# Fixed issue order on every engine, staged loads and software-pipelined slots in a fused linear-attention and gMLP block

## The chip, the cores and the metric

The kernel runs on one core of one Trainium2 chip. The metric is the device time of one execution in microseconds (us); lower is better. A *profile* is one execution with the hardware profiler on. Its *span* runs from the first to the last instruction. Executions come in two states: some are a few per cent longer than the fastest of the same kernel, whatever the kernel; those over 1.5% longer are called slow.

In the lines of the profile PE is TensorE (matmuls) and PEld its weight loads, DVE is VectorE, ACT ScalarE, POOL GpSimd and SP SyncE. A `q` after an engine's name, as in ACTq or SPq, marks an instruction that issues work from its queue, here DMA transfers. `out<-in` names the tiles, and L566 is line 566 of that run's kernel. A *bank* is a piece of PSUM, the memory that matmuls write; an *eviction* copies a result out of it. *Clock* is the granted TensorE clock as a share of full speed.

## The reference, cut to what matters

Sequence 2048, model width 448, 16 heads of 28, hidden width 896 for each half of the gMLP, all bf16.

```python
mod = (silu(c) @ w_mod)            # six vectors of 448: sa, ca, ga, sb, cb, gb
h = layernorm(x) * (1 + ca) + sa
q, k, v = split(h @ wqkv)
phi = lambda t: concat(softmax(t @ w_phi), softmax(-(t @ w_phi)))      # per head
kv, z = phi(k).T @ v, phi(k).sum(0)
x = x + ga * ((phi(q) @ kv / (phi(q) @ z + 1e-6)) @ wo)
h = layernorm(x) * (1 + cb) + sb
z1, z2 = split(gelu(h @ w_in)); z2 = layernorm(z2)
g = w_sp @ z2 + b_sp                # a 2048 x 2048 product over the sequence
x = x + gb * ((z1 * g) @ w_out)
```

## The kernel before

The sequence is cut into 16 tiles of 128 rows, and the program has four stages. The **start** loads the weights, computes silu(c) and the modulation vectors, and folds w_phi and (1 + ca) into the K weights; for this it lays w_phi out as a block-diagonal matrix, BD. The **K stage** computes k, v and the sum over phi(k) for each tile, and the q features in between. The **middle** goes through slots: `num` (attention numerator), `wo` (output projection, second norm), `z2` and `z1`. The **gate stage** multiplies by w_sp and w_out. Norms go as follows: VectorE computes mean and variance, GpSimd raises the variance to the power -1/2 (`rstd`), VectorE computes `nmr` = -mean * rstd, GpSimd applies both, and a DMA transpose makes the result a matmul operand (hT for the first norm, h2T for the second).

A scheduler orders the instructions of each engine; the program text gives only the dependences and a priority. The parts that matter, with cuts marked `# ...`:

```python
# head of the program: every load, from two queues
nc.scalar.dma_start(out=wm1[:], in_=wmod_v[:, :, 0:960])
nc.sync.dma_start(out=x_sb[:, 0:4, :], in_=xv[:, 0:4, :])
# ... Wv on SP; wk_raw and four blocks of BD on ScalarE
for st in range(1, NST):
    nc.sync.dma_start(out=x_sb[:, st * 4:(st + 1) * 4, :], in_=xv[:, st * 4:(st + 1) * 4, :])
load_rows(nc.scalar, wq_raw[:], A_wqkv[:, 0:D])
# ... wmg, wo_s, wm2 on ScalarE
load_rows(nc.scalar, win_s[:], B_w_in)
# ... wmg, wout_s on ScalarE
nc.scalar.dma_start(out=bsp[:], in_=B_b_sp.partition_broadcast(P))
# ...
nc.scalar.activation(out=e[:], in_=cT[:], func=ACT.Exp, scale=-1.0)      # the start of silu(c)

# PSUM: six single banks and one pair
def bank(name):  return psp.tile([P, 512], F32, name=name, tag="B", bufs=6)
def bank2(name): return psp.tile([P, 2, 512], F32, name=name, tag="A", bufs=1)

# middle
for j in range(NT + 7):
    if j < NT: num(j)
    # ... z1 of the tiles that are ready
    if 0 <= j - 2 < NT: wo(j - 2)          # ends with the second norm and its h2T transpose
    if 0 <= j - 4 < NT: z2(j - 4)          # two single banks, two gelus
    if 0 <= j - 5 < NT: z2norm(j - 5)
    if j >= NT:
        for n in ((j - NT) * 2, (j - NT) * 2 + 1):
            if n < 8: load_wsp(2 + n // 4, n % 4)    # w_sp pieces, transposed on the SP queue
```

Of the kernel before, what the change touches and what calls it, by code (L numbers as in the profile page):

```python
# [15 lines left out]
P = 128  # L16
D = 448
# [457 lines left out]
KD = [P, P, P, D - 3 * P]  # L475
HP = 4
# [4 lines left out]
def fast_path(tc, A_x, A_wqkv, A_w_phi, A_wo, B_w_in, B_w_sp, B_b_sp, B_w_out, c, w_mod, out, flag):  # L481


    nc = tc.nc
# [5 lines left out]
    wspA = tc.alloc_tile_pool(name="f_wspA", bufs=1)  # L490
# [3 lines left out]
    def bank(name):  # L494
        return psp.tile([P, 512], F32, name=name, tag="B", bufs=6)

    def bank_bf(name):
        return psp.tile([P, 1024], BF, name=name, tag="B", bufs=6)

    def bank2(name):  # L500
        return psp.tile([P, 2, 512], F32, name=name, tag="A", bufs=1)

    ident = persist.tile([P, P], BF, name="f_ident")
    make_identity(nc, ident[:])
# [8 lines left out]
    sbcol = persist.tile([P, KC], BF, name="f_sbcol")  # L513
    cb1 = persist.tile([P, KC], F32, name="f_cb1")
    xpad = [persist.tile([P, 512], BF, name=f"f_xpad{r}") for r in range(6)]
    opad = [persist.tile([P, 512], BF, name=f"f_opad{r}") for r in range(3)]
# [7 lines left out]
    wq_raw = aph.tile([P, KC, D], BF, name="f_wq_raw")  # L524
    BD = aph.tile([CB, 4, CB], BF, name="f_BD")
# [5 lines left out]
    vring = [aph.tile([P, H, DH + 1], BF, name=f"f_vaug{r}") for r in range(3)]  # L531

    sm = tc.alloc_tile_pool(name="f_sm", bufs=3)


    c_row = aph.tile([1, D], BF, name="f_c_row")
    nc.sync.dma_start(out=c_row[:], in_=c)
    xv = A_x[0].rearrange("(n p) d -> p n d", p=P)
    wmod_v = w_mod.rearrange("(k p) n -> p k n", p=DC)
    nc.scalar.dma_start(out=wm1[:], in_=wmod_v[:, :, 0:960])  # L540
    nc.sync.dma_start(out=x_sb[:, 0:4, :], in_=xv[:, 0:4, :])
# [4 lines left out]

    load_rows(nc.sync, Wv[:], A_wqkv[:, 2 * D:3 * D])
    nc.vector.memset(BD[:], 0.0)
    load_rows(nc.scalar, wk_raw[:], A_wqkv[:, D:2 * D])
    phiv = A_w_phi.rearrange("(g l) d f -> l d g f", l=4)  # L550
    with nc.allow_non_contiguous_dma(reason="small w_phi blocks"):
        for hl in range(4):
            nc.scalar.dma_start(out=BD[hl * DH:(hl + 1) * DH, :, hl * DH:(hl + 1) * DH], in_=phiv[hl])
    for st in range(1, NST):
        nc.sync.dma_start(out=x_sb[:, st * 4:(st + 1) * 4, :], in_=xv[:, st * 4:(st + 1) * 4, :])
    load_rows(nc.scalar, wq_raw[:], A_wqkv[:, 0:D])
    nc.scalar.dma_start(out=wmg[:, :, 0:D], in_=wmod_v[:, :, 2 * D:3 * D])
    load_rows(nc.scalar, wo_s[:], A_wo)
    nc.scalar.dma_start(out=wm2[:], in_=wmod_v[:, :, 3 * D:3 * D + 960])
    load_rows(nc.scalar, win_s[:], B_w_in)  # L560
    nc.scalar.dma_start(out=wmg[:, :, D:2 * D], in_=wmod_v[:, :, 5 * D:6 * D])
    nc.scalar.dma_start(out=wout_s[:], in_=B_w_out.rearrange("(k p) n -> p k n", p=P))
    nc.scalar.dma_start(out=bsp[:], in_=B_b_sp.partition_broadcast(P))


    nc.gpsimd.memset(mhalf[:], -0.5)  # L566
    for r in range(6):
        nc.gpsimd.memset(xpad[r][:, D:512], 0.0)
        nc.gpsimd.memset(xpad[r][:, D:D + 1], 1.0)
    for r in range(3):  # L570
        nc.gpsimd.memset(opad[r][:, D:512], 0.0)
        nc.gpsimd.memset(pring[r][:, 2 * D:2 * D + 16], 0.0)
        nc.gpsimd.memset(vring[r][:, :, DH:DH + 1], 1.0)
    nc.gpsimd.memset(Wq[:, :, D:D + 16], 0.0)
    sapad = aph.tile([P, KC, 65], BF, name="f_sapad")
    sbpad = persist.tile([P, KC, 65], BF, name="f_sbpad")
    nc.gpsimd.memset(sapad[:], 0.0)
    nc.gpsimd.memset(sbpad[:], 0.0)
    ones = aph.tile([P, 1], BF, name="f_ones")
    nc.gpsimd.memset(ones[:], 1.0)  # L580
    with nc.allow_low_precision("a 0/1 mask is exact in bf16"):
        nc.vector.tensor_reduce(out=mask[:], in_=ident[:].rearrange("p (k h) -> p h k", h=HP), axis=AX.X, op=ALU.add)
    for s in range(2):
        nc.vector.tensor_copy(out=KVbd[:, s, :, :, 29], in_=mask[:].unsqueeze(1).to_broadcast([P, 4, HP]))


    ct_ps = bank_bf("ct_ps")
    for kk in range(KC):
        nc.tensor.transpose(ct_ps[0:DC, 2 * kk:2 * kk + 1], c_row[0:1, kk * DC:(kk + 1) * DC], ident[0:1, 0:1])
    ctv = ct_ps[0:DC, 0:8].rearrange("p (k t) -> p k t", t=2)[:, :, 0]  # L590
    cT = aph.tile([DC, KC], F32, name="f_cT")
    nc.vector.tensor_copy(out=cT[:], in_=ctv)
    e = aph.tile([DC, KC], F32, name="f_e")
# [3 lines left out]
    scol = aph.tile([DC, KC], BF, name="f_scol")  # L597
    nc.vector.tensor_tensor(out=scol[:], in0=e[:], in1=cT[:], op=ALU.mult)  # L598

    def colform(wm, pad, one_plus, tagn):  # L600
        cf = bank("cf" + tagn)
        for j in range(8):
            jv, m = divmod(j, 4)
            for kk in range(KC):
                nc.tensor.matmul(cf[:, j:j + 1], lhsT=wm[:, kk, jv * D + m * P:jv * D + m * P + P],  # L605
                                 rhs=scol[:, kk:kk + 1], start=(kk == 0), stop=(kk == KC - 1))
        nc.vector.tensor_copy(out=pad[:, :, 64], in_=cf[:, 0:4])
        nc.vector.tensor_scalar(out=one_plus[:], in0=cf[:, 4:8], scalar1=1.0, scalar2=None, op0=ALU.add)
        nc.vector.memset(one_plus[64:65, 3:4], 1.0)

    ca1 = aph.tile([P, KC], F32, name="f_ca1")

    def fold_T(wraw, wT):
        for g in range(4):
            tps = bank_bf("tps")
            for m in range(KC):
                nc.tensor.transpose(tps[0:CB, m * P:m * P + KD[m]], wraw[0:KD[m], m, g * CB:(g + 1) * CB],
                                    ident[0:KD[m], 0:KD[m]])
            if g % 2 == 0:
                nc.vector.tensor_copy(out=wT[:, g, 0:D], in_=tps[0:CB, 0:D])  # L620
            else:
                nc.scalar.copy(out=wT[:, g, 0:D], in_=tps[0:CB, 0:D])

    def fold_W(wraw, wT, W):
# [5 lines left out]
        nc.vector.tensor_copy(out=wT[:, :, D], in_=sa_ps[0:CB, 0:4])  # L630
        for m in range(KC):
            M = P if m < 3 else 65
            pf = bank("pf")
            for g in range(4):
                nc.tensor.matmul(pf[0:M, g * CB:(g + 1) * CB], lhsT=wT[:, g, m * P:m * P + M], rhs=BD[:, g, :],
                                 start=True, stop=True)
            dst = W[0:M, m, 0:D].rearrange("p (g f h) -> p g h f", g=4, h=HP)
            srcv = pf[0:M, 0:D].rearrange("p (g h f) -> p g h f", g=4, h=HP)
            if m % 2 == 0:
                nc.scalar.activation(out=dst, in_=srcv, func=ACT.Copy, scale=ca1[0:M, m:m + 1])  # L640
            else:
                nc.vector.tensor_scalar(out=dst, in0=srcv, scalar1=ca1[0:M, m:m + 1], scalar2=None, op0=ALU.mult)

# [7 lines left out]

    xr = [0]

    def ln_tail(mv, n, src, idx, tagp, dst):

        rstd = sm.tile([P, 4], F32, tag=tagp + "rs")
        nc.gpsimd.tensor_scalar(out=rstd[:, 0:n], in0=mv[:, 0:n, 1], scalar1=LN_EPS, scalar2=None, op0=ALU.add)
        nc.gpsimd.tensor_tensor(out=rstd[:, 0:n], in0=rstd[:, 0:n], in1=mhalf[:, 0:n], op=ALU.pow)
        nmr = sm.tile([P, 4], F32, tag=tagp + "nm")
        nc.vector.scalar_tensor_tensor(out=nmr[:, 0:n], in0=mv[:, 0:n, 0], scalar=-1.0, in1=rstd[:, 0:n], op0=ALU.mult, op1=ALU.mult)  # L660
        for t in range(n):
            xp = xpad[xr[0] % 6]
            xr[0] += 1
            nc.gpsimd.tensor_scalar(out=xp[:, 0:D], in0=src(t), scalar1=rstd[:, t:t + 1], scalar2=nmr[:, t:t + 1],  # L664
                                    op0=ALU.mult, op1=ALU.add)
            nc.sync.dma_start_transpose(out=dst(t), in_=xp[:])  # L666

    def ln1(st):
        mv = sm.tile([P, 4, nc.vector.BN_AGGR_DIM], F32, tag="l1mv")
        for t in range(4):  # L670
            stats = sm.tile([P, nc.vector.BN_STATS_DIM], F32, tag="l1st")
            nc.vector.bn_stats(out=stats[:], in_=x_sb[:, st * 4 + t, :])
            nc.vector.bn_aggr(out=mv[:, t, :], in_=stats[:])
        ln_tail(mv, 4, lambda t: x_sb[:, st * 4 + t, :], None, "l1",
                lambda t: hT[:, :, (st * 4 + t) * P:(st * 4 + t + 1) * P])

    ln1(0)
    colform(wm1, sapad, ca1, "a")
    wT = aph.tile([CB, 4, D + 1], BF, name="f_wTk")
    fold_T(wk_raw, wT)  # L680
    bv = bias_row(sapad, Wv, 0, D)
    for kk in range(KC):
# [3 lines left out]
    fold_W(wk_raw, wT, Wk)  # L686
# [3 lines left out]
    kvacc = bank2("kvacc")  # L690

    def kv_proj(i):
        k_ps = bank("k_ps")
        v_ps = bank("v_ps")
        for kc in range(KC):
            K = P if kc < 3 else 65
            nc.tensor.matmul(k_ps[:, 0:D], lhsT=hT[0:K, kc, i * P:(i + 1) * P], rhs=Wk[0:K, kc, :], start=(kc == 0), stop=(kc == KC - 1))  # L697
        for kc in range(KC):
            K = P if kc < 3 else 65
# [312 lines left out]
```

## Time and profile before

| | before |
|---|---|
| timed runs, median (range) | 363.83 us (363.71 to 364.49) |
| profiled run | 372.96 us, span 371.1, state slow |
| first K matmul | 66.4 us |
| K stage, to the first `num` matmul | 66.4 us |
| middle, to the first w_sp matmul | 113.1 us |
| gate stage | 125.2 us |

The first K matmul is the first matmul of the first K tile: its k in the kernel before, its v in the changed one. The prediction below shows the strip of busy tenths, ScalarE's start and the table of stretches. One more view was used to check the stages, the list of what PE waited for: the waiting operation and its line, the releaser, then the total in us, the number of waits and the longest.

```profile
PE cfa L605 <- DVE f_scol L598: 54.2, 1, 54.2
PE num L829 <- DVE t L843: 10.6, 8, 3.5
PE x_ps L856 <- DMA oT<-f_opad: 7.6, 4, 3.1
PE z_ps L877 <- DMA h2T<-f_xpad: 4.3, 2, 2.9
```

The first line is the start: one wait of 54.2 us for silu(c). The second is the middle, where `num` has a single pair of banks and waits for VectorE to empty it.

### The profile page before, as it was taken

The numbers are of one execution on the slowest core, as the hardware profiler recorded it, in microseconds if no ns is written. First come the engines' busy times: TensorE is split into PE (matmuls) and PEld (weight loads), VectorE is DVE, ScalarE is ACT, GpSimd is POOL, SyncE is SP. The second block draws the span as 40 slices with busy tenths as digits, with TensorE's granted clock in tenths as the row PEclk, the third lists the DMA queues.
The fourth block names the chain that finished last, engine by engine and source line by source line (L and its number), as shares of the span: only waits on it lengthen the run. The fifth ranks groups of instructions, "written<-read, shape, count | busy, mean of one in ns | idle before, by whom it ended". The sixth has DMA issues, their size and how long they took to land. (4 is left out here: it accounts for less than half of the span.)

```text
span 371.1 us, 4240 instructions
## 1 busy us (share of the span) xinstructions
PE 275.0 (74%) x1506; PEld 134.6 (36%) x1528; DVE 174.0 (47%) x384; ACT 98.6 (27%) x206; POOL 100.3 (27%) x176
## 2 busy tenths in 40 slices
PE   0000008999969946897879795799999999999992
PEld 0000006665425522333334341244444444444440
DVE  1720003696726745667777764233443334444422
ACT  0000012677718751534445462240000000000000
POOL 2552400345940014754655554000000000000000
PEclk9999999999969996889999997799999999999997
DMA  8999899800000002412222279700000000000001
GB/s 229 269 208 208 166 218 238 108 2 1 2 0 0 2 0 42 73 34 53 42 44 56 42 154 208 165 5 0 0 2 25 25 2 25 25 2 12 27 12 56
DMA packets 69656, 25.81 MB, mean 70 GB/s; under 512 B 60473, under 2 KB 69050, under 8 KB 69626
## 3 DMA queue, kind: packets, MB, share of 16 engines
q1 hardware_dynamic: 64290, 18.76, 25.4%
q10 hardware_dynamic: 5336, 6.69, 8.2%
q8 instruction: 14, 0.23, 0.3%
q14 instruction: 16, 0.13, 0.1%
HBM read 8.92 MB, written 1.84 MB: 29 GB/s over the span
## 5 line engine op out<-in xcount | busy, mean ns | idle before, releaser
L932 PE MATMUL g_ps<-f_wsp,f_z2n 128*128 128x512 bf16 x437 | 98.2, 379 | 0.6
L932 PEld LDWEIGHTS <-f_z2n 128*128 128x128 bf16 x448 | 43.9, 98 | 52.2
L934 DVE TENSOR_TENSOR gb<-g_ps,f_bsp 128x512 f32<-128x512 f32 x28 | 19.4, 692 | 68.6 <-PE g_ps L932 68.6
L605 PE MATMUL cfa<-f_scol,f_wm 112*128 112x1 bf16 x32 | 1.0, 165 | 54.2 <-DVE f_scol L598 54.2
L877 PE MATMUL z_ps<-f_win,h2T 128*128 128x448 bf16 (+1 forms) x128 | 31.3, 391 | 4.3 <-DMA h2T<-f_xpad 4.3
L845 POOL TENSOR_TENSOR f_opad<-t 128x448 bf16<-128x448 bf16 x16 | 16.5, 1033 | 53.6 <-issue 30.4
L898 PE MATMUL z_ps<-h2T,f_win 128*128 128x512 bf16 (+1 forms) x106 | 27.9, 397 | 3.1 <-DMA h2T<-f_xpad 2.6
L664 POOL TENSOR_SCALAR f_xpad<-f_x,rstd,nmr 128x448 bf16<-128x448 bf16 x32 | 22.9, 721 | 21.8 <-DMA f_hT<-f_xpad 13.2
L856 PE MATMUL x_ps<-f_wo,oT 128*128 128x448 bf16 x64 | 18.9, 391 | 7.6 <-DMA oT<-f_opad 7.6
L880 DVE BATCH_NORM_STATS2 stats<-z2g 128x6 f32<-128x448 bf16 x32 | 19.4, 611 | 9.6 <-ACT z2g L879 9.6
L939 PE MATMUL o_ps<-f_wout,f_z1T 128*128 128x448 bf16 x112 | 23.3, 352 | 0.0
L707 DVE TENSOR_REDUCE sums<-f_E 128x32 f32<-128x896 bf16 x16 | 17.3, 1084 | 11.8 <-ACT f_E L703 11.6
L605 PEld LDWEIGHTS <-f_wm 112*128 112x128 bf16 x64 | 2.0, 100 | 54.4 <-issue 50.1
L879 ACT ACTIVATE z2g<-z_ps 128x448 bf16<-128x448 f32 x32 | 17.4, 544 | 14.6 <-PE z_ps L877 14.6
L899 ACT ACTIVATE f_z1T<-z_ps 128x512 bf16<-128x512 f32 x28 | 16.7, 597 | 14.5 <-PE z_ps L898 14.5
L935 DVE TENSOR_TENSOR f_z1T<-gb,f_z1T 128x512 bf16<-128x512 f32 x28 | 19.4, 692 | 1.7 <-DVE gb L934 0.5
L877 PEld LDWEIGHTS <-h2T 128*128 128x128 bf16 (+1 forms) x128 | 13.3, 107 | 17.8 <-DMA h2T<-f_xpad 5.4
L829 PE MATMUL num<-f_KVbd,f_Eq 112*128 112x120 bf16 x128 | 10.5, 232 | 12.3 <-DVE t L843 10.6
L843 DVE TENSOR_TENSOR t<-num,w 128x896 bf16<-128x896 f32 x16 | 17.4, 1087 | 0.4
L697 PE MATMUL k_ps<-f_Wk,f_hT 128*128 128x448 bf16 x64 | 16.6, 380 | 0.2 <-ACT f_Wk L640 0.2
L729 PE MATMUL q_ps<-f_hT,f_Wq 128*128 128x512 bf16 (+1 forms) x59 | 16.6, 396 | 0.3
L898 PEld LDWEIGHTS <-f_win 128*128 128x128 bf16 x112 | 10.9, 100 | 15.3 <-DMA h2T<-f_xpad 3.4
(111 smaller groups left out, 351.3 us busy)
## 6 DMA issues: line engine op xcount, KB each, us to landing
f_x<-in_A_x_dram SPq DMA_DIRECT2D x4, 448.0 KB, 7.0
out_dram<-ot SPq DMA_DIRECT2D x16, 112.0 KB, 1.7
f_wm<-in_w_mod_dram ACTq DMA_DIRECT2D x2, 840.0 KB
f_win<-in_B_w_in_dram ACTq DMA_DIRECT2D x1, 1344.0 KB, 13.3
f_wmg<-in_w_mod_dram ACTq DMA_DIRECT2D x2, 392.0 KB
f_wout<-in_B_w_out_dram ACTq DMA_DIRECT2D x1, 784.0 KB
f_bsp<-in_B_b_sp_dram ACTq DMA_DIRECT2D x1, 512.0 KB, 4.7
f_wk_raw<-in_A_wqkv_dram ACTq DMA_DIRECT2D x1, 336.0 KB, 7.9
```

The source lines that it names most:

```text
L664: nc.gpsimd.tensor_scalar(out=xp[:, 0:D], in0=src(t), scalar1=rstd[:, t:t + 1], scalar2=nmr[:, t:t + 1], op0=ALU.mult, op1=ALU.add)
L707: nc.vector.tensor_reduce(out=sums[:], in_=E[:].rearrange("p s (c f h) -> p (s c) h f", c=4, h=HP), axis=AX.X, op=ALU.add)
L843: nc.vector.tensor_tensor(out=t[:], in0=nv[:, :, :, 0:DH], in1=w[:].unsqueeze(3).to_broadcast([P, 2, H, DH]), op=ALU.mult)
L856: nc.tensor.matmul(x1[:, 0:D], lhsT=oT[0:KD[cc], cc, :], rhs=wo_s[0:KD[cc], cc, :], start=(cc == 0), stop=False)
L877: nc.tensor.matmul(z_ps[:, 0:D], lhsT=h2[0:K, kc, il * P:(il + 1) * P], rhs=win_s[0:K, kc, FH + hf * D:FH + (hf + 1) * D], start=(kc == 0) ...
L879: nc.scalar.activation(out=z2g[:, hf, :], in_=z_ps[:, 0:D], func=ACT.Gelu_apprx_tanh)
L880: nc.vector.bn_stats(out=stats[:, hf, :], in_=z2g[:, hf, :])
L898: nc.tensor.matmul(z_ps[:], lhsT=win_s[0:K, kc, fc * P:(fc + 1) * P], rhs=h2[0:K, kc, :], start=(kc == 0), stop=(kc == KC - 1))
L932: nc.tensor.matmul(g[:], lhsT=z2n[:, s_, fc * P:(fc + 1) * P], rhs=wsp_tiles[tcn][:, s_, :], start=(s_ == 0), stop=(s_ == NT - 1))
L934: nc.vector.tensor_tensor(out=gb[:], in0=g[:], in1=bsp[:, tsl], op=ALU.add)
L935: nc.vector.tensor_tensor(out=z1T[:, fc, tsl], in0=gb[:], in1=z1T[:, fc, tsl], op=ALU.mult)
L939: nc.tensor.matmul(o_ps[:, 0:D], lhsT=z1T[:, fc, t * P:(t + 1) * P], rhs=wout_s[:, fc, :], start=(fc == 0), stop=(fc == FC - 1))
```

## The change

The intent is to take the order out of the scheduler's hands: every engine gets its instructions in the order of the text, so that loads stand where they are needed, and each slot does work whose inputs were made a slot earlier. The diff, cut to its core:

```diff
+    with tc.manual_schedule():                      # around everything below
-    bank: bufs=6      bank2: bufs=1
+    bank: bufs=4      bank2: bufs=2
 # start: only what is needed first; table load ahead of the exponential
-    for st in range(1, NST):
-        nc.sync.dma_start(out=x_sb[:, st * 4:(st + 1) * 4, :], ...)
-    load_rows(nc.scalar, wq_raw[:], A_wqkv[:, 0:D])
-    ...                                             # wmg, wo_s, wm2, win_s, wmg, wout_s, bsp on ScalarE
+    nc.sync.dma_start(out=cT[:], in_=c.rearrange("o (k p) -> p (o k)", p=DC))    # c as columns
+    nc.scalar.activation(out=warm[:], in_=warm[:], func=ACT.Exp)
+    nc.vector.tensor_tensor(out=BD[:]..., in0=phi[:]..., in1=bmask[:]..., op=ALU.mult)   # BD by a mask
 # K stage
+    def loads(i):                                   # on SP, one or two per slot
+        if i == -1: x tiles 4-7, wq_raw
+        elif i == 0: x tiles 8-11, wmg ...
+        ...                                         # to i == 7: bsp
+    for i in range(NT):
+        q_exp of an earlier pair; k_mm(i)
+        l1_stats(i + 4); l1_rstd; l1_apply(i + 3, nc.gpsimd)
+        loads(i); k_norm(i); kv_acc(i - 2); late(i)
+        if i in QS: q_mm(QS[i])                     # two q chunks into a pair of banks
+        if 10 <= i < 14: load_wsp(0, i - 10)
 # middle
-    num(j); z1; wo(j - 2); z2(j - 4); z2norm(j - 5)
+    for j in range(NT + 8):
+        l2_apply(j - 4); num_fin(j - 1); z2_norm(j - 7); wo_mm(j - 3)
+        z2_stats(j - 6); z2_rstd(j - 6); l2_stats(j - 3); z2_mm(j - 5)
+        z1 units; num_mm(j)                         # z2_mm: two halves, a pair of banks, one gelu
+    for tcn in range(1, 4):                         # w_sp after the last h2T
+        for q in range(4): load_wsp(tcn, q)
```

Smaller parts: the folded weights are kept in an order that lets their evictions be contiguous, the second norm's statistics are read from PSUM instead of from the copy, and the scaling of wo and w_in moves from GpSimd to VectorE.

## The prediction

> **What bounds the kernel now.** I read the profile in this order: the forty-slice strip of busy tenths, the ScalarE timeline of the first 58 us, the table of stretches cut where the program changes stage, then the chain that ended last and VectorE's timeline inside one stage.
>
> The strip shows PE idle for the first six slices (9.3 us each) while the DMA engines are 80 to 90% busy, and again thinner in the middle:
>
> ```profile
> PE   0000008999969946897879795799999999999992
> DMA  8999899800000002412222279700000000000001
> ```
>
> The ScalarE timeline says why PE starts so late. All of ScalarE's loads stand ahead of its first computation, exp(-c), and everything PE needs (the modulation columns, then the folded K weights) hangs on that exponential:
>
> ```profile
> 24.80 0.39 ACTq L544 DMA_DIRECT2D f_win<-in_B_w_in_dram  x1
> 40.49 0.47 ACTq L545 DMA_DIRECT2D f_win<-in_B_w_in_dram  x1
> 54.25 0.36 ACTq L563 DMA_DIRECT2D f_bsp<-in_B_b_sp_dram  x1
> 54.64 1.28 ACT L594 ACT_TABLE_LOAD   x1 [54.64 <-DMA f_hT<-f_xpad]
> 55.93 0.21 ACT L594 ACTIVATE f_e<-f_cT 112x4 f32<-112x4 f32 x1
> ```
>
> The reader is to see the gap from 24.80 to 40.49 between two issues: the built program makes a load wait for the transfer eight issues earlier, so the queue advances only as data lands. c itself was in the chip at 2.0 us and the first modulation weight at 6.6 us.
>
> The stretches (fold, K stage, attention/MLP stage, its drain, spatial gate) give each engine's busy time:
>
> ```profile
> 56.50:66.40 9.90, 9.37 (x84) 7.05 (x84) 3.74 (x13) 2.90 (x5) 0.61 (x1) 1.00 1.09 212
> 66.40:132.80 66.40, 61.85 (x428) 33.73 (x433) 42.61 (x66) 44.90 (x88) 27.37 (x23) 0.95 0.10 13
> 132.80:211.50 78.70, 58.50 (x335) 27.41 (x339) 53.62 (x153) 33.83 (x86) 41.57 (x71) 0.91 0.23 44
> 211.50:245.90 34.40, 27.30 (x108) 11.13 (x109) 15.12 (x40) 14.88 (x28) 11.84 (x26) 0.85 0.70 146
> 245.90:371.10 125.20, 117.48 (x550) 54.74 (x559) 47.48 (x72) 0.60 (x1) 0.00 (x0) 0.98 0.05 16
> ```
>
> First figure after the bounds is the length, then PE, PEld, DVE, ACT, POOL busy, the granted clock, DMA share, GB/s. The K stage is PE's (93%). The gate stage is PE's too and nothing in it can be hidden better. The middle is nobody's: PE 74%, VectorE 68%. In it a slot repeats every 5.66 us; VectorE works about 4.35 of that and waits twice for GpSimd's power:
>
> ```profile
> 201.19 0.16 DVE L660 SCALAR_TENSOR_TENSOR nmr<-mv,rstd 128x1 f32<-128x1 f32 x1 [0.73 <-POOL rstd L658]
> 203.12 0.51 DVE L890 TENSOR_SCALAR f_z2n<-z2g,mv,rstd 128x896 bf16<-128x896 bf16 x1 [0.58 <-POOL rstd L885]
> 206.85 0.16 DVE L660 SCALAR_TENSOR_TENSOR nmr<-mv,rstd 128x1 f32<-128x1 f32 x1 [0.73 <-POOL rstd L658]
> ```
>
> The drain is stalled by the queue: small h2T transposes stand on SP behind the big f_wsp ones, and the chain that ended last runs through them:
>
> ```profile
> 229.41 0.04 issue
> 229.45 2.04 SPq L738
> 231.49 0.04 issue
> 231.53 2.13 SPq L738
> ...
> 233.76 2.83 DMA h2T<-f_xpad
> ```
>
> **What the Trainium skill says.** "TensorE: Matmul & The Clock Gate", § Architectural detail, says ScalarE and VectorE are strict first-in first-out. The trace agrees: the table load starts at 54.64, straight after the last issue (54.25 + 0.36). The same page, § What's actually happening, gives PE half rate until about 3.4 us of sustained work and again after an idle window. The trace agrees: in the first K tile 448-column matmuls start 0.37 us apart (66.73 to 67.10), in a steady one 0.19, and the granted clock is 0.50 in 140 to 145 us, after an idle gap. "DMA: Bandwidth & Descriptors", § Issuing engines are not separate DMA queues, says loads started by different engines share the same 16 DMA engines. So moving loads from ScalarE to SP buys no bandwidth (218 GB/s over the first 56 us); it can only free ScalarE and change the order.
>
> **The change part by part**, in the profiled run's time, by stage.
>
> 1. *Start.* ScalarE keeps four issues of its present kind for wm1 and wk_raw, and its table load is moved ahead. c comes as columns, so four transposes go. Before K tile 0 only about 2.1 MB must land; at 218 GB/s that is about 10 us, and wk_raw, early in it, about 8 us (in the profile it took 7.9 us behind a load of twice the size). From there the fold costs what it costs now, 9.9 us: about 18 us for the first K matmul instead of 66.4. **Gain 48 us.**
>
> 2. *K stage.* PE's work is the same: 16 tiles of k, v (8 x 0.19 = 1.5 us) and accumulation (0.42), 64 q matmuls (14 us), folds, gates, bias rows and norms: about 57 us at full clock. The 4.0 us for which PE now waits around 101 to 107 us for the squares on GpSimd go, and q exponentials are paired. Against that, VectorE carries per slot statistics 0.75, sum 1.1, reciprocal 0.35, product 0.8: 3.0 us, plus about 7 us of scaling moved from GpSimd. Banks fall from six single ones to four and evictions wait in VectorE's order, so in slots 1 to 3, with the fold of q, K tile i+1 waits for tile i's exponentials (1.3), normalisation (2.3) and eviction: about 5 us each. The loads for this stage, 6.7 MB and 1.2 MB of transposes, need 36 us at 218 GB/s, and slots 0 to 12 last about 45: close, not binding. Working: slots 0 to 3 20 us, 4 to 11 8 x 3.2 + 2, 12 to 15 13.5, the tail with the last norms and q 7: **68 us, against 66.4: loss 2 us.** It ends near 86.
>
> 3. *Middle.* Two pair banks instead of one let num run ahead. But the order is fixed, and VectorE's last item in a slot (second-norm statistics) releases GpSimd's add and power (0.22 + 0.57 + hand-overs, about 1.05 us), which releases VectorE's first item in the next. VectorE's own starts-to-starts in the slot add to 4.5 us. Slot: 4.5 + 1.05 = **5.55 us, against 5.66**. Fill until slot 7 goes at that pace: num, VectorE chain 2, add 1.05, transpose 2.5 and so on, 23 us. Then 9 slots of 5.55 = 50; slots 16 to 19 without num 5.5 + 3.6 + 3.5 + 3.7 = 16; the last z2 and z1(3), seven units of four matmuls at 0.22, 8.5: **98 us, against 113.1: gain 15 us.** Most of it is the drain, since every h2T transpose now precedes the f_wsp ones.
>
> 4. *Gate stage.* 448 x 0.219 + 112 x 0.19 = 119 us and a 6 us ending: unchanged, 125 us. The twelve late f_wsp pieces take 2.1 to 2.8 us each; four are needed by +24 us and arrive by +11. **0 us.**
>
> Sum: 371.1 - 48 + 2 - 15 = 310 us profiled. The three timed runs are 363.83/371.1 = 0.980 of the profiled span: **304 us**.
>
> **Rivals.** (a) *DMA is the real start bound.* For it: 12.2 MB moved in 56 us at 90% busy, so the loads are not shortened. Against: only 2.1 MB is needed first, and the rest is wanted over 60 us. If K slots 4 to 11 ran at the pace of their loads (4.3 us each, 0.9 MB at 218 GB/s), about 9 us more: 313. (b) *The fixed order makes VectorE and GpSimd the bound.* For it: the 1.05 us ring closes once in every slot, and any second wait, such as a statistic waiting for ScalarE's copy, adds directly; at 6.3 us a slot, 0.75 x 11 = 8 us more: 312. Against: the scheduler's own order waits twice as it is. (c) *Better than my bank-stall estimate.* If the fold slots cost 3.5 us and PE stays at full clock, K takes 58 and the time is 294. (d) *f_wsp1 late*, because its space is freed late or the piece is slow: at most the time by which four pieces exceed 24 us, 0 to 5 us; the pieces of now speak against it.
>
> **Range and chances.** The start's gain is sure to about 5 us; K may be off by 10 either way, the middle by 10, the last by 3. As independent errors that is about 15 us: 304, 290 to 320. Even with (a) and (b) together the time is 321, so faster by over 2% is nearly certain: 0.98, same 0.01, slower 0.01.
>
> **What would show it.** Right: the first K matmul at 16 to 22 us, exp(-c) by 6; the first num matmul at 80 to 92; nums 5.4 to 5.7 us apart in steady slots, with VectorE's nmr waiting about 1 us for the power; the f_wsp pieces after the last h2T; a last stage of 124 to 127 us. Wrong: if K tiles start more than 3.6 us apart in slots 4 to 11 with PE waiting on hT or loads, (a) holds and my bandwidth sum failed; if slots are above 6 us, (b). If K tiles in slots 1 to 3 follow in under 4 us, my bank argument fails and the time is under 298. A start later than 25 us would mean small loads (c as columns, w_phi) land late.

## The result, and the profile after

The changed kernel takes 319.06 us (median of 4 runs, 317.58 to 320.70), against 364.16 (363.71 to 371.13, 4 runs, one of them slow) before. The ratio is 0.877, with a 95% interval of 0.871 to 0.882. Ratios here are the mean time of one kernel's fast runs over that of the other's fast runs of the same rounds, so they are not quite the ratio of the medians.

The profile of before was a slow run. So before was profiled again as the first experiment (363.53 us, span 361.6), and this is what the changed profile (317.58 us, span 315.7, fast) is compared with:

| stage, us | before, slow profile | before, again | changed | change against "again" |
|---|---|---|---|---|
| start, to the first K matmul | 66.4 | 55.7 | 20.7 | -35.0 |
| K stage | 66.4 | 66.1 | 67.0 | +0.9 |
| middle | 113.1 | 112.5 | 102.4 | -10.1 |
| gate stage | 125.2 | 127.3 | 125.6 | -1.7 |
| span | 371.1 | 361.6 | 315.7 | -45.9 |

The strip of the changed kernel (each digit is the busy share of a fortieth of the span, in tenths):

```profile
PE   0699799899738677788777899999999999999991
DMA  6454898459202321241222199990000000000001
```

PE now works from the second slice on, and the DMA engines are half busy at first where they were 80 to 90% busy. The table of stretches, with the same columns as in the prediction; the middle is cut here where the last `num` matmul starts, which is a little earlier than the cut by eye made of before:

```profile
0.00:20.70 20.70, 9.65 (x85) 7.20 (x86) 6.48 (x28) 5.93 (x11) 6.64 (x38) 1.00 0.50 129
20.70:87.70 67.00, 60.52 (x428) 32.95 (x433) 51.10 (x103) 43.62 (x74) 23.07 (x33) 1.00 0.70 157
87.70:160.00 72.30, 53.53 (x322) 25.97 (x325) 54.16 (x147) 29.04 (x69) 40.91 (x68) 0.95 0.23 46
160.00:190.10 30.10, 24.94 (x122) 11.17 (x123) 19.90 (x48) 14.89 (x25) 17.75 (x33) 1.00 0.44 86
190.10:315.70 125.60, 117.81 (x550) 54.71 (x559) 47.57 (x72) 0.60 (x1) 3.73 (x4) 0.98 0.24 53
```

The start moves 129 GB/s where before moved 218: it is short because fewer bytes precede the first matmul. The prediction cites the Trainium skill that loads of different queues share the same DMA engines; no run here tests whether another queue brings bandwidth. The clock column needs care: it also shows 1.00 where the trace has no clock record. The first record is at 24.9 us in the changed kernel (70.2 in before), and the 448-column matmuls ahead of it start 0.37 us apart, half the pace of the 0.19 afterwards. The middle's main part still has no full engine (PE 53.5 of 72.3, VectorE 54.2).

ScalarE's start, and VectorE in two steady slots (start, duration, instruction, and in brackets what it waited for):

```profile
5.88 0.34 ACTq L566 DMA_DIRECT2D f_wm<-in_w_mod_dram  x1
6.24 1.28 ACT L573 ACT_TABLE_LOAD   x1 [6.24 <-DMA f_wm<-in_w_mod_dram]
7.54 0.20 ACT L573 ACTIVATE f_warm<-f_warm 128x1 f32<-128x1 f32 x1
7.65 0.19 ACT L595 ACTIVATE f_e<-f_cT 112x4 f32<-112x4 bf16 x1
```

```profile
147.49 0.16 DVE L611 SCALAR_TENSOR_TENSOR nmr<-l2mv,rstd 128x1 f32<-128x1 f32 x1 [1.12 <-POOL rstd L609]
...
153.28 0.16 DVE L611 SCALAR_TENSOR_TENSOR nmr<-l2mv,rstd 128x1 f32<-128x1 f32 x1 [1.12 <-POOL rstd L609]
```

The exponential comes at 7.65 instead of 55.93. The table load was written ahead of it, but stands behind ScalarE's four load issues all the same, the last of them at 5.88. The two `nmr` are 5.79 us apart, and 1.12 us of that is VectorE waiting for GpSimd: VectorE works 4.67 us a slot. What PE waited for:

```profile
PE z_ps L960 <- DMA h2T<-f_xpad: 13.6, 14, 1.6
PE tps L639 <- DMA f_wk_raw<-in_A_wqkv_dram: 7.9, 1, 7.9
...
PE pf L658 <- DVE f_BD L692: 2.5, 1, 2.5
PE q_ps L753 <- DVE f_Wq L663: 2.4, 1, 2.4
```

The 54.2 us for silu(c) are gone. In their place stand 7.9 us for the K weights, a 2.5 us wait for the block-diagonal BD and a 2.4 us wait in K slot 4 for one chunk of folded Wq; both of the last two stand in VectorE's fixed order behind other work. `num` waits 6.7 us in the middle where it waited 12.2 over all releasers (the 10.6 above are VectorE's share), and z2 waits for its h2T fourteen times.

### The profile page after: what moved, and what is told of

Read it like the earlier page. It is cut to its first block, busy times and chain, and to the rows that moved or that the text cites. A ratio compares the mean times of both kernels' runs of the same rounds, so it can differ in the third digit from the quotient of the medians.

```text
span 315.7 us, 4217 instructions
## 1 busy us (share of the span) xinstructions
PE 266.4 (84%) x1500; PEld 132.0 (42%) x1524; DVE 179.2 (57%) x395; ACT 94.1 (30%) x179; POOL 92.1 (29%) x174
## 5 line engine op out<-in xcount | busy, mean ns | idle before, releaser
L1037 DVE TENSOR_TENSOR gb<-g_ps,f_bsp 128x512 f32<-128x512 f32 x28 | 19.4, 692 | 69.4 <-PE g_ps L1035 67.4
L960 PE MATMUL z_ps<-f_win,h2T 128*128 128x448 bf16 (+1 forms) x128 | 27.1, 354 | 13.6 <-DMA h2T<-f_xpad 13.6
L990 PE MATMUL z_ps<-h2T,f_win 128*128 128x512 bf16 (+1 forms) x106 | 25.6, 379 | 0.3
L928 POOL TENSOR_TENSOR f_opad<-t 128x448 bf16<-128x448 bf16 x16 | 18.4, 1151 | 23.8 <-DVE t L926 19.3
L963 ACT ACTIVATE z2g<-z_ps 128x896 bf16<-128x896 f32 x16 | 14.7, 917 | 30.7 <-PE z_ps L960 26.6
L960 PEld LDWEIGHTS <-h2T 128*128 128x128 bf16 (+1 forms) x128 | 11.2, 97 | 27.1 <-DMA h2T<-f_xpad 17.8
L759 ACT ACTIVATE f_Eq<-q_ps 112x1024 bf16<-112x1024 f32 x16 | 16.2, 1024 | 13.2 <-PE q_ps L753 13.1
L753 PE MATMUL q_ps<-f_hT,f_Wq 128*128 128x512 bf16 (+1 forms) x57 | 14.8, 379 | 4.8 <-DVE f_Wq L663 2.4
L969 DVE BATCH_NORM_STATS2 stats<-z2g 128x6 f32<-128x448 bf16 x32 | 18.3, 615 | 0.1
L720 PE MATMUL v_ps<-f_Wv,f_hT 128*128 128x448 bf16 x64 | 16.2, 379 | 1.0 <-DMA f_hT<-f_xpad 0.9
L990 PEld LDWEIGHTS <-f_win 128*128 128x128 bf16 x112 | 10.9, 97 | 12.8
L1042 PEld LDWEIGHTS <-f_z1T 128*128 128x128 bf16 x112 | 11.0, 98 | 11.8 <-issue 1.0
```

Source lines behind the costliest of these rows:

```text
L928: nc.gpsimd.tensor_tensor(out=op_[:, 0:D], in0=t[:, 0].rearrange("p h d -> p (h d)"), in1=t[:, 1].rearrange("p h d -> p (h d)"), op=ALU.add)
L960: nc.tensor.matmul(z_ps[:, hf, 0:D], lhsT=h2[0:KB[kc], kc, il * P:(il + 1) * P], rhs=win_s[0:KB[kc], kc, FH + hf * D:FH + (hf + 1) * D], s ...
L969: nc.vector.bn_stats(out=stats[:, hf, :], in_=z2gs[i][:, hf, :])
L990: nc.tensor.matmul(z_ps[:], lhsT=win_s[0:KB[kc], kc, fc * P:(fc + 1) * P], rhs=h2[0:KB[kc], kc, :], start=(kc == 0), stop=(kc == KC - 1))
L1037: nc.vector.tensor_tensor(out=gb[:], in0=g[:], in1=bsp[:, tsl], op=ALU.add)
L1042: nc.tensor.matmul(o_ps, lhsT=z1T[:, fc, t * P:(t + 1) * P], rhs=wout_s[:, fc, :], start=(fc == 0), stop=(fc == FC - 1))
```

## The experiments

**Theory.** The gain is the start (loads no longer ahead of the exponential) and the end of the middle (w_sp pieces no longer ahead of the h2T transposes); a steady slot is set by the ring VectorE, GpSimd, VectorE, and neither the pairs of banks nor the order as such matter much. **Rivals:** the fixed order is itself worth most of it; the pairs let PE run ahead; other rings are close behind. All twelve kernels computed the right result. The stages below are from each run's profile (us); the times are medians over all runs. The runs fell on four chips: e0 to e3 on one, e4 to e6 and e8 on another, e7, e9 and e10 on a third, e11 on a fourth. The fast runs of the kernel before range from 360.8 to 370.7 us over them, so what follows rests on stages and waits in profiles more than on times a few us apart.

| kernel | time | ratio to before, 95% interval | start | K | middle | gate |
|---|---|---|---|---|---|---|
| changed | 319.06 | 0.877 (0.871 to 0.882) | 20.7 | 67.0 | 102.4 | 125.6 |
| e1, loads up front | 335.95 | 0.920 (0.913 to 0.928) | 38.7 | 67.7 | 102.3 | 125.4 |
| e9, e1 and two w_sp pieces | 337.56 | 0.923 (0.913 to 0.933) | 40.3 | 66.6 | 102.4 | 125.5 |
| e11, e9 and all hT first | 341.82 | 0.944 (0.931 to 0.957) | 49.2 | 63.3 | 102.8 | 125.1 |
| e2, before with staged loads | 345.14 | 0.946 (0.938 to 0.953) | 28.8 | 73.7 | 114.2 | 126.5 |
| e4, scheduler's order | 326.20 | 0.896 (0.878 to 0.913) | 23.8 | 61.6 | 111.8 | 125.8 |
| e5, nmr on GpSimd (one of six slow) | 309.92 | 0.848 (0.833 to 0.862) | profile slow | | | |
| e3, no nmr | 312.78 | 0.858 (0.852 to 0.864) | 20.8 | 68.2 | 95.2 | 126.1 |
| e6, z2 not paired | 318.83 | 0.874 (0.859 to 0.889) | 20.8 | 68.2 | 102.3 | 125.8 |
| e7, w_sp among h2T | 326.33 | 0.892 (0.881 to 0.903) | 20.7 | 66.9 | 110.9 | 125.6 |
| e8, four edits (four of six slow) | 309.28 | 0.851 (0.835 to 0.867) | 20.0 | 66.5 | 89.8 | 125.5 |
| e10, five edits | 305.22 | 0.834 (0.824 to 0.844) | 19.6 | 67.9 | 89.5 | 125.5 |

### e0: before again

No edit.

> The kernel before, unchanged, for a second profile. Its first profile fell in a slow run (span 371.1 us) while its timed runs are near 364, and the prediction scaled by 0.980 on the belief that profiled spans are longer than timed runs. Theory: the scale was wrong because that one run was slow, by a lower granted clock of PE in the K stage and the middle; a fast run gives a span of 361 to 363 with those two stages 5 to 10 us shorter in all and the gate stage unchanged. Rival: profiling itself lengthens this kernel, and the span is again 369 to 372.

It took 363.53 us with a span of 361.6. The difference to the slow profile lies in the start (55.7 against 66.4), not in the stages where the expectation looked for it; the K stage and the middle are the same within 0.7 us, and the gate stage is 2.1 longer. And the timed value is the span plus 1.9 us: the prediction's factor of 0.980 was the step from a slow run to fast ones, not a property of profiling. Two lines of SP and three of ScalarE in this profile (queue issues; x12 means twelve of a kind in a row):

```profile
20.47 2.12 SPq L738 DMA_TRANSPOSE f_wsp<-in_B_w_sp_dram  x1
22.69 19.30 SPq L666 DMA_TRANSPOSE f_hT<-f_xpad  x12
```

```profile
22.42 0.39 ACTq L544 DMA_DIRECT2D f_win<-in_B_w_in_dram  x1
34.94 0.47 ACTq L545 DMA_DIRECT2D f_win<-in_B_w_in_dram  x1
37.15 0.38 ACTq L561 DMA_DIRECT2D f_wmg<-in_w_mod_dram  x1
```

From 22.7 to 42.0 SP issues twelve hT transposes that the scheduler pulled forward, and in the same stretch ScalarE's loads stand still for 12.1 us. The semaphore records of the trace say more: in each of three places a load issue of ScalarE starts just after an hT transpose of the *other* queue has landed (22.40, then 22.42; 34.92, then 34.94; 43.57, then 43.59). The slow profile has the same pairs, at 24.80, 40.49 and 54.25. So the suspicion is that the loads wait for these transposes; e11 tests it.

### e1: the changed kernel with its loads up front

```diff
     load_rows(nc.sync, Wv[:], A_wqkv[:, 2 * D:3 * D])
+    x tiles 4-15 on SP; wq_raw, wmg, wo_s, wm2, win_s, wmg, wout_s, bsp on ScalarE
 def loads(i):
+    return
```

> The changed kernel with one part undone: all loads again stand at the head of the two queues, the late weights on ScalarE ahead of exp(-c). Theory (most of the gain is ScalarE's queue no longer standing behind loads): the first K matmul moves from 20.7 us to 42 to 60, and the time to 340 to 358. Rival (the gain comes from the fixed order of the engines): within 5 us of the changed kernel, 315 to 324.

It took 335.95 us (2 runs), 17 more than the changed kernel. The exponential moves from 7.65 to 25.68 us and the first K matmul from 20.7 to 38.7: both by 18.0. Nothing else moves by more than 0.7. So staging the loads is worth 18 us, less than half of what the prediction put on the start. The first K matmul (42 to 60 expected) and the time (340 to 358) both came below the expectation, and the other 17.0 us up to 55.7 in the kernel before had to have another cause.

### e9: and two w_sp pieces among the loads

```diff
+    load_wsp(0, 0)        # right after SP's loads of x
     l1_apply(3, nc.gpsimd)
+    load_wsp(0, 1)
```

> The kernel with all loads up front (335.95 us; first K matmul at 38.7 us) with two f_wsp pieces moved among the loads, as the scheduler had them in the kernel before. Theory (they are what delays the start of the kernel before from 38.7 to 55.7 us): first K matmul at 44 to 50 us, 341 to 348 us. Rival (the pieces fit beside the loads, and the rest of the difference is the order of the other loads, the table load and the exponential behind ScalarE's issues): first K within 2 us of 38.7, 334 to 338 us.

337.56 us and a first K matmul at 40.3: 1.6 us, not the 5 to 11 of the theory. In this run only the first piece stood among the loads, issued at 10.26 us; the second was issued at 39.0, after the exponential at 27.24. So one piece fits beside the loads, and two were not tested. As far as it was tested, the theory fell.

### e11: and all sixteen first norms with their hT transposes ahead

```diff
+    for q in range(NT // 2):
+        l1_stats(2 * q); l1_stats(2 * q + 1); l1_rstd(q)
+        l1_apply(2 * q, eng); l1_apply(2 * q + 1, eng)
     e + 1; reciprocal; scol          # silu's chain, after them on VectorE
     ...
-        l1_stats(i + 4); l1_rstd; l1_apply(i + 3, nc.gpsimd)      # in the K slots
```

> The kernel with all loads up front and two f_wsp pieces among them (337.56 us; first K matmul at 40.3 us) with all sixteen first norms and their hT transposes done before the exponential's chain, as the kernel before has them. Theory (the transposes of the whole of x among the loads are what delays ScalarE's later loads, its last issue at 20.6 us here against 43.6 in the kernel before, and with it the exponential): last load issue of ScalarE at 36 to 44 us, first K matmul at 48 to 57 us, K stage 2 to 5 us shorter as the norms are out of it, 343 to 352 us. Rival (the fine-grained block loads of w_phi on ScalarE and the order of the others make the difference): last issue before 25 us, first K at 38 to 44 us, 333 to 339 us.

The first K matmul is at 49.2, and ScalarE's issues halt at the same load as in e0:

```profile
18.84 0.38 ACTq L556 DMA_DIRECT2D f_win<-in_B_w_in_dram  x1
27.73 0.47 ACTq L557 DMA_DIRECT2D f_win<-in_B_w_in_dram  x1
30.89 0.33 ACTq L582 DMA_DIRECT2D f_wmg<-in_w_mod_dram  x1
35.93 0.38 ACTq L583 DMA_DIRECT2D f_wout<-in_B_w_out_dram  x1
...
37.39 1.28 ACT L588 ACT_TABLE_LOAD   x1 [37.39 <-DMA f_hT<-f_xpad]
```

In e9 the same two halves of the w_in load were issued at 17.68 and 18.23, and the last load at 20.61; here it is 36.99, inside the 36 to 44 expected. So with the sixteen transposes pulled ahead the loads of the other queue are late, and with them the exponential (38.79 instead of 27.24): 8.9 us at the start, of which 3.3 come back because the K stage has no norms left. The time (341.82) is 1.2 us under the expected range.

The trace shows how. The built program gives the transfers of both queues eight completion semaphores in turn, and an issue waits until the transfer that last held its semaphore has landed. Four load issues of e11 start 0.02 to 0.03 us after an hT transpose landed: 27.71, then 27.73; 30.86, then 30.89; 35.91, then 35.93; 36.97, then 36.99. So it is a wait that the built program puts in, and not shown to be a shortage of bandwidth. Two things stay open. The second w_sp piece, issued at 39.0 in e9, here stands among the transposes (26.82, 4.19 us), and its share of the 8.9 us is not separated. And the last 6.5 us up to 55.7 are not split; they are there already in ScalarE's last load issue (43.6 in e0, 37.0 here). The kernel before has four small block loads of w_phi on ScalarE, which take 4.5 us to issue, and other differences.

### e2: the kernel before with staged loads alone

```diff
-    loads of x tiles 4-15, wq_raw, wmg, wo_s, wm2, win_s, wmg, wout_s, bsp at the head
+    def loads(i): ...      # as in the change, called in the K loop
```

> The kernel before with one part alone: the late loads leave ScalarE's queue and are issued on SP stage by stage, the tile scheduler still sets the order. Theory: the first K matmul falls from 66.4 to 20 to 26 us and the time to 318 to 330, so this part alone gives most of the change. Rival (fixed order): above 350.

345.14 us (2 runs): the start falls to 28.8 (-26.9), but the K stage grows to 73.7 (+7.6). The expectation missed both the first K matmul (20 to 26) and the time (318 to 330), and the rival (above 350) did not hold either. With the scheduler's order, staging earns 18 us of the 45 by itself. Of the 7.6 us of the K stage 4.7 are lost in the first three tiles (16.2 us until the fourth begins, 11.5 in e0), which run at half rate. The same four matmuls, first in e2, 6 us after the first K matmul, then in e0, 5 us after it:

```profile
34.62 1.68 PE L687 MATMUL k_ps<-f_Wk,f_hT 128*128 128x448 bf16 x4
```

```profile
60.71 0.93 PE L697 MATMUL k_ps<-f_Wk,f_hT 128*128 128x448 bf16 x4
```

In e2 the full-rate clock record begins at 43.5, 14.7 us after the first K matmul; in e0 at 59.1, 3.4 us after it. Why e2 stays at half rate so long is not shown. Another 2.5 us are slot 10 (12.53 against 10.03), where PE waits for the squares on GpSimd: 6.3 us in the stage against 3.8.

### e4: the changed kernel in the scheduler's order

```diff
-    with tc.manual_schedule():
+    if True:
```

> The changed kernel with one line changed: the scheduler is free to order the instructions again; loads, pairs, lags and arithmetic stay as written. Theory (the middle is set by the VectorE-GpSimd ring and not by the order; the order is worth what it does for the loads at the start): first K matmul 21 to 30 us, middle 98 to 108 us, 315 to 328 us in all. Rival (the fixed order itself is worth much in the K stage and the middle): middle over 110 us or K stage over 72, above 332 us. Second rival (the fixed order costs time in the middle): slots below 5.5 us and under 312 us in all.

326.20 us, inside the theory's range; but its stages do not follow the theory. The start is 3.1 us later, the K stage 5.4 us *shorter*, and the middle 9.4 us longer, which was the rival's mark. So the fixed order is worth about 7 us in all (7.1 against the changed kernel, 7.4 against e6, which ran on the same chip in the same rounds and is as fast): a loss in the K stage and a gain in the start and the middle. In the K stage slot 4 takes 3.67 instead of 6.26 us, as the scheduler does not put the folded Wq chunk behind other work, and slot 10 takes 3.67 instead of 5.26. In the middle VectorE's waits differ (same columns as PE's list), first for the scheduler's order, then for the fixed one:

```profile
DVE nmr L611 <- POOL rstd L609: 12.1, 14, 1.7
DVE f_z2n L983 <- POOL rstd L978: 8.7, 12, 1.0
DVE stats L969 <- ACT z2g L963: 7.3, 4, 2.5
```

```profile
DVE nmr L611 <- POOL rstd L609: 18.0, 16, 1.3
DVE f_z2n L983 <- POOL rstd L978: 3.0, 3, 1.0
```

The scheduler spreads VectorE's waits over three releasers, 28.1 us in the middle; the fixed order has little but the one for each tile, 21.0. But these waits alone do not explain the 9.4 us. By place, 2.4 of them are in the drain (32.5 against 30.1), where the scheduler put six w_sp pieces among the last h2T transposes, as e7 does; 8.0 are in the first eight slots (39.2 against 31.2), where the granted clock is also lower up to 113 us (0.69 against 0.87); and the last seven slots are 1.0 *shorter* (40.1 against 41.1). This is read from the traces; none of it was tested alone.

### e5: nmr on GpSimd

```diff
-        rstd, nmr = rstd_of(mv2.pop(i), 1, "l2")        # nmr on VectorE
+        rstd by add and power on GpSimd, as before
+        nc.gpsimd.tensor_scalar(out=nmr, in0=mean, scalar1=rstd, scalar2=-1.0, op0=ALU.mult, op1=ALU.mult)
```

> The changed kernel with -mean*rstd of the second norm computed on GpSimd right after the power, so VectorE no longer waits for GpSimd at that place; the application keeps its cheap mult-add form (0.75 us). Theory (a slot is VectorE's 4.67 us plus 1.12 us of waiting for the power): slots of 4.5 to 4.9 us, middle 10 to 12 us shorter, 307 to 311 us. Rival (another ring of GpSimd, transposes and PE is close behind): slots of 5.2 to 5.6 and a time of 313 to 318 us.

309.92 us (6 runs), 9.1 less than the changed kernel, and 8.9 less than e6, which ran on the same chip in the same rounds and is as fast as the changed kernel. Steady slots are 4.83 us where they were 5.80: the saving is 0.97 of the 1.12 us that VectorE waited, and GpSimd pays 0.26 us for the product. The theory of the ring holds. The profiled run was slow (314.22): two slots before the steady ones took 7.33 and 7.13 us, with an h2T 2.6 us late and PE's clock down afterwards. So this run's stages are not compared; the spacing of 4.84 in the steady slots of e8's and e10's fast profiles is the same.

### e3: no nmr at all

```diff
+        nc.gpsimd.tensor_scalar(out=xp[:, 0:D], in0=x_sb[:, i, :], scalar1=mean, scalar2=rstd,
+                                op0=ALU.subtract, op1=ALU.mult)          # was x * rstd + nmr
```

> The changed kernel with the second norm applied as (x - mean) times rstd on GpSimd, so VectorE's first instruction of each slot, which waits for GpSimd's power, is gone. Theory (a slot is VectorE's own 4.67 us plus a wait of 1.12 us in a ring VectorE, GpSimd, VectorE): slots fall from 5.79 to 4.6 to 4.9 us and the time by 9 to 15 us, to 304 to 310. Rival (PE's wait for the h2T transpose is the bound and VectorE's wait only fills it): slots stay above 5.5 and the time within 4 us.

312.78 us: 6.3 less, where 9 to 15 were expected. The slots do fall to 4.83, but the form of the application matters. The groups of GpSimd work in e3, then in the changed kernel (busy us, then ns for one):

```profile
L956 POOL TENSOR_SCALAR f_xpad<-f_x,l2mv,rstd 128x448 bf16<-128x448 bf16 x16 | 31.1, 1944 | 1.7
```

```profile
L616 POOL TENSOR_SCALAR f_xpad<-f_x,rstd,nmr 128x448 bf16<-128x448 bf16 x30 | 22.6, 757 | 8.9 <-DVE nmr L611 3.1 <-ACT z2g L963 2.2 <-issue 1.8
```

Subtract-and-multiply takes 1.94 us where multiply-and-add of the same shape takes 0.76. GpSimd is then full for the whole slot: 2.02 + 1.03 + 0.23 + 0.57 + 0.22 + 0.56 = 4.63 us of work in 4.83. That this costs the rest of the expected gain is argued, not shown: the steady slots are as short as e5's. Against the changed kernel the last seven slots gain 5.4 us and the drain 2.9, while the first eight slots lose 1.1, the K stage, which the edit does not touch, 1.2, and the gate stage 0.5. e5, which keeps the cheap form, is 2.9 us faster by the medians, though the intervals of the two ratios overlap.

### e6: z2 in two single banks

```diff
-        z_ps = bank2("z2_ps");  one gelu over both halves
+        for hf in range(2): z_ps = bank("z2_ps");  a gelu for each half
```

> The changed kernel with z2 as two single-bank units with two gelu activations, so one part of the pairing is undone. Theory (VectorE and its wait set the slots, ScalarE has room): within 3 us of the changed kernel, 316 to 322 us. Rival (pairing is what lets z2 run ahead): nums over 6.1 us apart and 324 us or more.

318.83 us, the same as the changed kernel. Pairing z2 buys nothing here. (The pairing of q and the second pair for `num` were not undone.)

### e7: w_sp pieces among the last h2T transposes

```diff
+        if NT <= j < NT + 6:
+            load_wsp: two pieces per slot
-    for tcn in range(1, 4): for q in range(4): load_wsp(tcn, q)      # after the last h2T
```

> The changed kernel with the twelve late f_wsp transposes issued two per slot among the last h2T transposes, as the kernel before had some of them, in place of after the last h2T. Theory (an h2T stands 2 to 4 us longer on the queue behind two big pieces, and PE in the drain waits for each h2T): the part from the last num matmul to the gate stage grows from 30.1 us to 36 to 42, 325 to 331 us in all. Rival (the big pieces fit into the gaps between the h2T transposes): at most 3 us more.

326.33 us, 7.3 more. From the last `num` to the gate stage it takes 38.7 us where the changed kernel takes 30.1: inside the expected 36 to 42. SP's queue and PE in the drain of e7:

```profile
175.15 4.12 SPq L764 DMA_TRANSPOSE f_wsp<-in_B_w_sp_dram  x2
179.36 1.21 SPq L618 DMA_TRANSPOSE h2T<-f_xpad  x1
180.62 4.67 SPq L764 DMA_TRANSPOSE f_wsp<-in_B_w_sp_dram  x2
185.38 1.21 SPq L618 DMA_TRANSPOSE h2T<-f_xpad  x1
```

```profile
177.39 1.95 PE L960 MATMUL z_ps<-f_win,h2T 128*128 128x448 bf16 x8 [3.09 <-DMA h2T<-f_xpad]
179.12 3.37 PE L990 MATMUL z_ps<-h2T,f_win 128*128 128x512 bf16 x8
```

An h2T stands behind two big pieces, PE waits 3.09 us for it, and then its next eight matmuls take 3.37 us where the same eight take 1.90 elsewhere in this drain: the wait also costs half the clock for a while. The order on this one queue is worth 8.5 us. e7 is not an exact undoing: it puts twelve pieces among the transposes, where the kernel before has eight among its last h2T. In e0's drain PE waits 7.5 us for two h2T where the changed kernel waits 5.1, and the drain gained 6.1 us (36.2 to 30.1) of the middle's 10.1. So e7 shows that the order matters by this much, and fits a drain gained by it.

### e8 and e10: edits together

e8 is e5 with three more edits, and e10 adds a fifth.

```diff
+    BD product ahead of l1_stats(0)                 # PE waited 2.5 us for it
-            fold_pf(wTq, Wq, 2, 1)                  # Wq chunk 2 evicted by VectorE: PE waited 2.4 us
+            fold_pf(wTq, Wq, 2, 0)                  # by ScalarE
+        if j >= NT: z1 units, then z2_mm(j - 5)     # drain: z1 ahead, while h2T is on its way
 # e10 only
+    one_plus(colform(wm1, 1), ca1)                  # ahead of l1_stats(2), l1_stats(3)
```

> The changed kernel with four edits together: -mean*rstd of the second norm on GpSimd; the block-diagonal product of w_phi moved ahead of the first statistics on VectorE (PE waits 2.50 us for it at the start); the eviction of one Wq chunk on ScalarE instead of VectorE (PE waits 2.42 us for it in slot 4); z1 ahead of z2 in the drain slots (PE waits 1.5 us each for h2T there). Theory: -10, -2, -2 and -4 us, 299 to 304 us. Rival (the small waits are hidden and only the ring counts): 307 to 311 us.

> The kernel with four edits (fast runs 303.65 and 307.16, the others 309 to 311) with a fifth: the modulation column 1 + ca ahead of the second pair of statistics on VectorE, because PE waited 2.0 us for it at the start where it had waited 2.5 us for the block-diagonal product before. Theory: first K matmul at 18.0 to 18.8 us instead of 20.0, K and later stages unchanged, fast runs 301 to 306 us. Rival (the next wait takes its place, as the column took that of the product): first K at 19.5 to 20.3, same time.

e8's two fast runs took 303.65 and 307.16 us; four more, of 309 to 311, count as slow. So one run of six lies in the theory's 299 to 304, and the median, 309.28, in the rival's 307 to 311. e10 took 305.22 (4 runs, 304.18 to 307.04). Both beat the changed kernel by their ratios. Neither is shown to beat e5: e8's interval overlaps e5's almost whole, and e10's four runs, all below e5's fastest of 308.93, ran on another chip, and the intervals overlap too. The ratio for e8, 0.851, does not follow from its two fast runs: their mean over that of the two fast runs of before there is 0.837. In e8's profile the middle is 89.8 us: the last `num` to the gate stage takes 24.5 us, without a PE wait, where the changed kernel takes 30.1. (e3, without z1 ahead, takes 27.2 there; z1 ahead was not run alone.) The edits at the start are worth little. With BD ahead, PE waits at the next place of VectorE's order, and with that mended, at one more; the lists of PE's waits in e8 and in e10:

```profile
PE cf L669 <- DVE f_ca L674: 2.0, 1, 2.0
```

```profile
PE b_ps L680 <- ACT f_Wk L661: 1.3, 1, 1.3
...
PE cf L669 <- DVE f_ca L674: 0.5, 1, 0.5
```

The first K matmul comes at 20.7, 20.0 and 19.6: 1.1 us in all for two waits of 2.5 and 2.0. For e10 that is the rival's 19.5 to 20.3, not the theory's 18.0 to 18.8. The K stage keeps its length too (67.0, 66.5, 67.9), though slot 4 of e8 takes 3.67 instead of 6.26: slots 5 and 6 take 3.64 and 4.19 where they took 2.70 and 3.67, with PE waiting for hT. e10's interval overlaps e8's, so the fifth edit is not shown to gain anything.

## Why the prediction was right or wrong

The direction is right and 319.06 lies inside 290 to 320, at its edge. It is 15 us low. The sum of stages (310.1 us of profiled span) is 5.6 below the 315.7 measured. The factor of 0.980 takes off 6.1 where 1.9 had to be added: another 8.0. And the profiled run is the fastest of the four, 1.5 below their median. 5.6 + 8.0 + 1.5 = 15.1.

1. **Start: mechanism right, size off.** Loads ahead of the exponential were a cause, and e1 shows it: it delays the exponential and the first K matmul by the same 18.0 us. "Gain 48" measured 35.0. Of the 13 missing, 10.7 are the slow profile's own (e0), and 2.3 are the changed start, 20.7 against 18.4. The weights came at 7.9 as predicted; the fold after them took 12.8 us instead of 9.9, and 2.5 of that is a wait for BD that the sum had not. The exponential, at 7.65 instead of "by 6", was not what held PE, which waited for wk_raw until 7.92. The prediction also named only ScalarE's loads. e0 and e11 show a second part: those loads wait, through the shared semaphores, for the hT transposes of the other queue; e11 has 8.9 us for it, with the w_sp piece in it.
2. **K stage: size right, by cancelling errors; the bank argument failed.** The predicted parts were 20, 27.6 and 20.5 us for slots 0 to 3, 4 to 11 and the rest; measured 14.3, 30.4 and 22.3. In slots 0 to 3 PE is busy 13.9 of 14.3 us, and waits for no bank; slots 1 and 2 take 4.2 us, nearly all of it PE's own work. What the sum missed is slot 4, where PE waits 2.4 us for a Wq chunk that stands behind other work on VectorE.
3. **Middle: mechanism right, terms mis-sized.** "4.5 + 1.05 = 5.55 us" measured 4.67 + 1.12 = 5.79 (just above the 5.4 to 5.7 it gave as a sign), and e5 confirms the ring by removing it (4.83). From the first to the last `num` it is 72.3 us where the prediction's parts give 23 + 8 x 5.55 = 67.4. From the last `num` on, its 5.55 + 16 + 8.5 = 30.1 is what was measured; that the sum meets it to a tenth is luck. The gain was 10.1 instead of 15, and 6.1 of it is the drain. Its claim that most of the gain is the order of h2T and w_sp agrees with that, and e7 is consistent with it.
4. **Gate stage: right.** 125.6 against 125. The w_sp pieces arrive in time.
5. **The step from profile to time: wrong.** The profile was slow and the timed runs fast, and 372.96 for the profiled run stood beside it.
6. **The clock of the first K tile: misread.** The prediction takes its half rate for the effect of an idle window. But PE had been busy 9.37 of the 9.90 us before it, and the half rate lasted until 70.2 us; the 1.00 in its table for those 9.90 us is a stretch without a clock record. Nothing in its sum hangs on this.

Of the rivals, (a) is not seen: in the K stage PE waits 0.9 us for hT and 0.2 us for a load. (b) is not seen: the ring's one wait of 1.12 us a slot is there, but no second one adds to it, and a slot is 5.80, not 6.3. (c) is right for the fold slots, 14.3 / 4 = 3.6 us each, but the time under 298 did not follow: slots 4 to 15 and the tail take 4.6 us more than predicted. (d) is not seen.

What stays open: the last 6.5 us of the old start and the w_sp piece's share in e11; why the scheduler's first eight slots are 8.0 us longer; why e2 stays at half rate; the pairs of q, the second pair for `num` and the lags between the slots, none of which was undone alone; and why e8 has so many slower runs.

## What to carry to other kernels

Look first at what stands ahead of the first computation on the engine that everything waits for, including work on *other* queues that a scheduler pulled forward: loads, transposes and big late weights belong where they are needed, and small transposes that PE waits for go ahead of big ones. Ask of each load's issue which landing it waits for, on the other queue too. In a fixed order, look for a value that goes to another engine and back within a slot, and give the whole round trip to one engine; but price the new instruction form in a profile first, and expect a removed wait that has another right behind it to give back only a part. Check the profiled run before scaling anything by it.

## What the Trainium skill lacked or had wrong

- "GPSIMD Engine Reference", § 4.1 Engine selection, says a one-input elementwise operation on GpSimd is roughly line-rate, without a difference by operation. Here multiply-and-add with two per-row scalars on 128x448 took 0.757 us and subtract-and-multiply of the same shape 1.944 us (e3).
- "TensorE: Matmul & The Clock Gate", § What's actually happening, ties the return to half rate to an idle window of about 3.4 us. In five of these traces (before, e0, changed, e7, e2) the clock records fall to half rate 26 times, and each fall follows 3.41 us in which PE was busy for between 0.0 and 1.65 us; with 1.69 us or more it kept full rate there. So a thinly used window was enough, without full idleness. e4 is less sharp: it fell after 1.81 and 1.89 us and stayed after 1.79. Some matmul records may be missing from a trace, so these are rough bounds.
- No page has the difference between the span from the first to the last instruction and the timed value: in the fourteen profiled runs it was 1.8 to 2.1 us for spans from 301.8 to 371.1, a constant and not a factor.
